# A gated mix of a state-space layer and attention on one core: where VectorE's share of the exponentials is taken from

## The chip, the cores and the metric

The kernel runs on one core of one Trainium2 chip. The metric is the device time of one execution in microseconds (us); the median of three runs is 934.88 (934.81 to 934.90). Its engines are TensorE (PE in the profile, its weight loads PEld), ScalarE (ACT), VectorE (DVE), GpSimd (POOL) and SyncE (SP), which here issues DMAs. Each works through a queue of its own in a fixed order and waits for the others by semaphores.

## The reference

One input `x` of 2048 rows by 1024 columns goes through two layers, and a gate mixes them row by row:

```
x = A_x
g = sigmoid((x * gate_w).sum(-1))            # one number per row
a = 2 Re(C h_t) + x * Dskip,  h_t = Lam_bar * h_(t-1) + B_bar x_t   # complex state, 1024 channels, 2048 steps
q, k, v = split(x @ wqkv)                    # 32 heads of 32
b = softmax(q k^T / sqrt(32)) v @ wo         # no mask
out = g * a + (1 - g) * b
```

Attention has 32 x 2048 x 2048 scores, about 134 million exponentials; they concern this case. Inputs and output are bf16.

## The kernel before

**Bursts.** The 32 heads are worked in 8 groups of four. A group has 8 units, one for each 256 queries, and a unit has 8 bursts, one for each 256 keys: 512 bursts in all. `burst(B)` (L1565 on) writes out one burst. One TensorE operation (QK, L1575) makes the scores of four heads: eight matmuls, for each head two key tiles of 128 keys by 256 queries, transposed so that keys lie on the partitions. A head's 512 columns (key tile 0, then key tile 1) fill one PSUM bank. Banks 0 to 5 are three slots of two banks (names `("S", 0)` to `("S", 2)`); burst number p takes the slots 2p mod 3 and 2p+1 mod 3, the first for heads 0 and 1, the second for heads 2 and 3. The scores of burst p+1 are therefore written over those of the first half of burst p and of the second half of burst p-1, and QK waits until both have been read.

ScalarE turns each half of a burst into exponentials with one ACTIVATE of 1024 columns (L1593) and writes them in bf16 to SBUF (`pt`, and in the opening other tiles that are still free). The numbers are not shifted by a maximum. The value matmuls (`pv`, L1649) follow about two bursts later: for each head, key tile and half of the queries one matmul of 33 columns into bank 6 (32 value columns and one of ones, which gives the sums). They are counted in quarters of a burst, of four matmuls each. After a unit's last quarter `normalize` (L1662, L1663) divides on VectorE.

**VectorE's share.** In some bursts VectorE computes part of the exponentials by bit arithmetic: a multiply and a clamp of the scores into a fixed-point number (`x_in`, L1584), a cubic in its fraction by three operations (`x_q`, L1614, L1615, L1611), and on GpSimd a last multiply and add whose 16-bit result is the bit pattern of the bf16 exponential (`x_p`, L1612). Two bursts make a batch: of bursts 0 and 2, or 4 and 6, of a unit, VectorE takes the last 256 columns of the fourth head, that is its key tile 1. ScalarE's second ACTIVATE is then of 768 columns (L1590), and waits for `x_in`, since both read the same bank. `x_in` stands directly behind QK in the written order; the three operations and GpSimd's come later, out of a list `xbg`. Two extra value operations (`x_pv`, L1629) multiply the batch's 512 columns, at burst 7 of the unit for bursts 0 and 2, at burst 1 of the next unit for bursts 4 and 6. `X_PLAN` names the 72 places, each a multiple of four bursts, at which a batch starts; the first is burst 148.

**What else TensorE does.** Beside attention it has the projections (L1402, L1420), the state-space layer's input product (`u`, L1432), its output product (`c`, L1461, with a diagonal matmul for `Dskip`, L1467) and the output projection (L1492). These dense chains use bank 7, one chain at a time; VectorE empties it at a chain's end (an evacuation). The state-space recurrence itself runs on VectorE as scans (L1349) between elementwise operations.

**The order.** A loop in `build` (from L1734) walks through the bursts and writes every queue in advance. In each burst it puts down QK and the exps, the quarters of value matmuls that are due, about four dense matmuls, and VectorE's background work. For that it keeps an estimate of VectorE's time (`dve_t`) against the burst's planned start `t0`; a burst is planned at 1.83 us, less 0.12 after one in which VectorE takes columns. Work from `xbg` goes ahead of other background work (`bg`, `bg2`) where it can start about as early. What does not end by a limit is left to the next burst. All this is fixed when the kernel is built; on the chip only semaphores decide.

The lines below are those that the diff touches and what calls them.

Of the kernel before, what the change touches and what calls it, by code (L numbers as in the profile page):

```python
# [6 lines left out]
BF = mybir.dt.bfloat16  # L7
F32 = mybir.dt.float32
# [923 lines left out]
RING = 60  # L932
C_LOADS = 28

X_AT = ((0, 2), (4, 6))
X_PLAN = (148, 152, 156, 160, 164, 168, 172, 176, 180, 184, 188, 192, 196, 200, 204, 208, 212, 216, 220, 224, 228, 232, 236, 240, 244, 248, 252, 256, 260, 296, 300, 304, 308, 312, 316, 320, 324, 328, 332, 360, 364, 368, 372, 380, 392, 396, 400, 404, 408, 412, 416, 420, 424, 428, 432, 436, 440, 444, 448, 452, 456, 460, 464, 468, 472, 476, 480, 484, 488, 492, 496, 500)
X_COLS = 256
X_A = SCALE * math.log2(math.e) * 65536.0
X_LO = -127.0 * 65536.0
E3, E2, E1, E0 = 0.0780245226404788, 0.2260671649, 0.6958335355, 0.9999252185627155  # L940
# [13 lines left out]
class FastPath:  # L954

    def __init__(self, nc, S, es, d, flag):
# [28 lines left out]
        self.xi = T("xi", [128, 2 * X_COLS], I32)  # L985
        self.xq = T("xq", [128, 2 * X_COLS], F32)
        self.xp = T("xp", [128, 2 * X_COLS], BF)
# [83 lines left out]
    def begin(self):  # L1071
        S, d = self.S, self.d
        pool, dve, act = self.pool, self.dve, self.act
        warm = self.hpb[0][:, 0, 0, :]
        dve(lambda e: e.memset(warm, 0.0), [], ["warm"])
        self.ld_w(0, 1, "act")
        self.ld_x(0)
        self.ld_w(0, 0, "act")
        for i, nm in enumerate(["A_Lambda_re", "A_Lambda_im", "A_log_dt", "A_Dskip", "gate_w"]):
            self.dma(lambda e, i=i, nm=nm: e.dma_start(self.prow[8 * i:8 * i + 8], d[nm].rearrange("(a p) -> a p", p=128)),  # L1080
                     [], [("prm", i)], "ld_prm", "act")
        for i in range(1, 8):
# [4 lines left out]
        pool(lambda e: e.memset(self.ones, 1.0), [], [("xp", 0)])  # L1087
        pool(lambda e: e.memset(self.badb[:, 1:2], 1.0), [], ["one"])
        pool(lambda e: e.affine_select(self.ident[:], self.ones, pattern=[[1, 128]], base=0, channel_multiplier=-1,
                                       compare_op=ALU.is_equal, fill=0.0), [("xp", 0)], ["ident"])  # L1090
# [472 lines left out]
    def burst(self, B):  # L1563
# [15 lines left out]
        mine = self.x_of.get(B)  # L1579
        first = None  # L1580
        if mine is not None:
            b, n = mine
            s = sl[1]
            first = self.dve(lambda e: e.tensor_scalar(self.xi[:, X_COLS * n:X_COLS * (n + 1)], ps[:, 2 * s + 1, 512 - X_COLS:512], X_A, X_LO, ALU.mult, ALU.max),  # L1584
                             [("S", s)], [("xi", n)], "x_in")
        for z in range(2):
            s, p = sl[z], self.pt_of(B, z)
            if z == 1 and first is not None:
                flat = lambda ap: ap.rearrange("p h n -> p (h n)")[:, 0:1024 - X_COLS]
                self.S.op("act", lambda e, s=s, p=p: e.activation(flat(self.tile[p]), flat(ps[:, 2 * s:2 * s + 2, :]), ACT.Exp, scale=SCALE),  # L1590
                     reads=[("S", s)], writes=[("pt", p)], deps=[first], name="exp")
            else:
                self.act(lambda e, s=s, p=p: e.activation(self.tile[p], ps[:, 2 * s:2 * s + 2, :], ACT.Exp, scale=SCALE), [("S", s)], [("pt", p)], "exp")  # L1593

    def x_plan(self, U, pair):
        self.x_when.setdefault(8 * U + (7 if pair[1] < 4 else 9), []).append(len(self.x_batch))
        for n, i in enumerate(pair):
            self.x_of[8 * U + i] = (len(self.x_batch), n)
        self.x_batch.append([8 * U + i for i in pair])

    def x_ops(self, b):
# [6 lines left out]
        i2, p2 = [("xi", 0), ("xi", 1)], [("xp", 0), ("xp", 1)]  # L1608
# [5 lines left out]
        return [(0.66, 0.0, lambda: self.dve(lambda e: e.scalar_tensor_tensor(xq[:], lo, E2 / E3 * w, lo, ALU.add, ALU.mult), i2, ["xq"], "x_q")),  # L1614
                (0.7, 0.0, lambda: self.dve(lambda e: e.scalar_tensor_tensor(xq[:], xq[:], E1 / E3 * w * w, lo, ALU.add, ALU.mult), ["xq"] + i2, ["xq"], "x_q")),  # L1615
                (0.7, 0.0, last)]

    def x_pv(self, b):

        ps, V = self.ps, self.V  # L1620
        for n, B in enumerate(self.x_batch[b]):
            U, i = divmod(B, BURSTS)
            g = U // QUNITS

            def mm(e, n=n, i=i, g=g):
                m = None
                for qt in range(2):
                    o = 33 * (4 * qt + 3)
                    m = e.matmul(ps[:, 6, o:o + 33], self.xp[:, X_COLS * n + 128 * qt:X_COLS * n + 128 * (qt + 1)], V[:, g % 2, 2 * i + 1, 3, :],  # L1629
                                 start=False, stop=False, skip_group_check=True)  # L1630
                return m
            self.S.op("pe", mm, reads=[("xp", n), ("V", g % 2, i // 2), "v1"], acc=["O"], name="pvx")

    def pv(self, q0, q1):

        ps, V = self.ps, self.V
        for q in range(q0, q1):
# [4 lines left out]

            def mm(e, B=B, z=z, p=p, kl=kl, i=i, g=g):
                m = None
                for h2 in range(1 if z == kl == 1 and B in self.x_of else 2):
                    for qt in range(2):
                        h = 2 * z + h2
                        o = 33 * (4 * qt + h)
# [28 lines left out]
    def build(self):  # L1677
# [13 lines left out]
        self.xbg, self.x_done = [], set()  # L1691
        self.opening()

        S.tok_w["O"] = S.tok_w[("bank", 6)]
# [37 lines left out]
        for p in range(first, NBURST):  # L1732
# [2 lines left out]
            self.p = p  # L1735
            if p > first:
                t0 += period
            if p % 4 == 0 and p in X_PLAN:
                self.x_plan(p // 8, X_AT[p // 4 % 2])
            while p in self.x_of and len(self.xbg) > 1:  # L1740
                self.xbg.pop(0)[2]()
            self.burst(p)
            period = PERIOD - (0.12 if p - 1 in self.x_of else 0.0)
            if p in self.x_of:
                self.dve_t = max(self.dve_t, t0 + 0.45) + 0.42
                b, n = self.x_of[p]
                if n == 1:
                    self.xbg += [[c, wait, f] for c, wait, f in self.x_ops(b)]
            q0, q1 = self.quarters[p]

            def values():
                self.pv(q0, q1)
                for b in self.x_when.get(p, ()):
                    while b not in self.x_done:
                        self.xbg.pop(0)[2]()
# [300 lines left out]
```

## Time and profile before

| | |
|---|---|
| median of three runs | 934.88 us |
| the profiled execution | 934.42 us |
| its span in the profile | 932.7 us |
| ScalarE busy | 916.7 us (98%), 1034 instructions |
| TensorE busy | 886.7 us (95%) |
| its weight loads | 501.7 us (54%) |
| VectorE busy | 718.8 us (77%) |
| GpSimd busy | 56.1 us (6%) |
| granted TensorE clock, mean | 0.998 |

How to read the lines that follow. A row of the groups is a source line, an engine, an operation and the tiles it writes and reads; after the shapes stand the count, then the busy time and the mean length of one in ns, and behind the second bar the engine's idle time just before and what ended most of it. Tiles carry the prefix `f_`. A row of a timeline has start and length in us; neighbours of one kind are merged (x3), so start plus length is the end of the last. Matmul ends are modelled, and a busy TensorE is not one at its peak. An ACTIVATE's row may start before the one ahead of it has ended, since the engine works on both at once.

### The profile page before, as it was taken

What the parts mean: (1) busy time and instruction counts of PE and PEld (TensorE: products, weight loads), DVE (VectorE), ACT (ScalarE), POOL (GpSimd) and SP (SyncE); (2) the same over time, 40 slices, a digit from 0 to 9 for tenths busy, and PEclk for the clock granted to TensorE, in tenths of its full rate; (3) what the DMA queues carried; (4) which work ended last, traced back from release to release, by engine and by line L of the source; (5) the groups of instructions that cost most, each with busy time, mean ns of one, the idle gap of its engine ahead of it and who ended that gap; (6) DMA issues with size and microseconds to landing.
All of it is one profiled execution on the core that took longest, in us unless ns stands there. A gap on an engine that the chain in (4) does not pass through costs nothing.

```text
span 932.7 us, 33715 instructions
## 1 busy us (share of the span) xinstructions
PE 886.7 (95%) x15095; PEld 501.7 (54%) x15316; DVE 718.8 (77%) x1457; ACT 916.7 (98%) x1034; POOL 56.1 (6%) x112
## 2 busy tenths in 40 slices
PE   8899999999999999999999999999999999989995
PEld 4555744464445565555655555544655655545553
DVE  2788888899888999886689965688898655676663
ACT  6999999999999999999999999999999999999997
POOL 2000000000000101100100010100000000001000
PEclk9999999999999999999999999999999999999999
DMA  9559433410233002130022501125201112323312
GB/s 201 96 101 139 76 53 76 84 30 27 42 64 84 31 8 51 41 86 29 8 41 51 86 16 41 42 62 98 42 16 41 53 50 63 121 84 121 119 62 74
DMA packets 157093, 60.90 MB, mean 65 GB/s; under 512 B 145680, under 2 KB 145680, under 8 KB 156944
## 3 DMA queue, kind: packets, MB, share of 16 engines
q1 hardware_dynamic: 154784, 58.16, 28.3%
q8 instruction: 121, 1.98, 0.9%
q10 hardware_dynamic: 2160, 0.53, 0.3%
q14 instruction: 28, 0.23, 0.1%
HBM read 16.79 MB, written 12.58 MB: 31 GB/s over the span
## 4 chain that ended last, share of the span: by engine, by line
ACT 74%; PE 19%; DVE 4%; SPq 1%; issue 1%; DMA 1%; DVEq 0%
ACT f_pt L1593 60%; ACT f_pt L1590 6%; PE f_ps L1461 6%; PE f_ps L1649 4%; PE f_ps L1575 4%; ACT f_OT L1593 2%; ACT f_Et L1593 2%; ACT f_cT_re L1593 2%; ACT f_cT_im L1593 2%; PE f_ps L1420 1%; PE f_ps L1402 1%; SPq L1052 1%; PE f_ps L1432 1%; DVE f_xi L1584 1%; DMA f_xT<-in_A_x_dram 1%
## 5 line engine op out<-in xcount | busy, mean ns | idle before, releaser
L1593 ACT ACTIVATE f_pt<-f_ps 128x1024 bf16<-128x1024 f32 x800 | 757.0, 1154 | 1.0 <-PE f_ps L1575 0.6
L1649 PEld LDWEIGHTS f_ps<-f_V,f_pt 128*128 128x128 bf16 x7264 | 224.0, 96 | 95.4 <-issue 68.4
L1649 PE MATMUL f_ps<-f_V,f_pt 128*128 128x33 bf16 x7264 | 260.1, 178 | 0.4 <-ACT f_pt L1593 0.4
L1575 PE MATMUL f_ps<-f_Q,f_K 32*128 32x256 bf16 x4096 | 203.4, 273 | 19.5 <-ACT f_pt L1593 8.3
L1575 PEld LDWEIGHTS f_ps<-f_Q,f_K 32*128 32x128 bf16 x4096 | 60.8, 92 | 161.6 <-ACT f_pt L1593 134.3
L1590 ACT ACTIVATE f_pt<-f_ps 128x768 bf16<-128x768 f32 x144 | 126.3, 877 | 0.6 <-DVE f_xi L1584 0.5
L1432 PE MATMUL f_ps<-f_xT,f_wb 128*128 128x512 bf16 x448 | 117.7, 379 | 6.3 <-issue 1.1
L1402 PE MATMUL f_ps<-f_xT,f_wb 128*128 128x512 bf16 x406 | 106.7, 379 | 3.9 <-issue 0.2
L1612 POOL TENSOR_SCALAR f_xp<-f_xq 128x512 int16<-128x512 f32 x72 | 46.1, 640 | 617.5 <-DVE f_xq L1611 433.4
L1584 DVE TENSOR_SCALAR f_xi<-f_ps 128x256 int32<-128x256 f32 x144 | 60.7, 422 | 28.7 <-PE f_ps L1575 26.0
L1349 DVE TENSOR_TENSOR_SCAN f_ht<-f_pf,f_init,f_ut 128x512 bf16<-128x512 f32 x64 | 81.0, 1279 | 0.0
L1461 PE MATMUL f_ps<-f_cT_im,f_hp 128*128 128x512 bf16 x192 | 72.6, 378 | 3.1
L1432 PEld LDWEIGHTS f_ps<-f_xT,f_wb 128*128 128x128 bf16 x512 | 40.0, 96 | 38.9 <-issue 7.8
L1420 PE MATMUL f_ps<-f_wb,f_xT 128*128 128x128 bf16 x896 | 59.3, 219 | 0.0
L1492 PE MATMUL f_ps<-f_wb,f_OT 128*128 128x512 bf16 x186 | 55.0, 380 | 2.9 <-DVE f_Et L1498 0.9
L1402 PEld LDWEIGHTS f_ps<-f_xT,f_wb 128*128 128x128 bf16 x464 | 36.1, 96 | 35.7 <-issue 8.0
L1461 PE MATMUL f_ps<-f_cT_re,f_hp 128*128 128x512 bf16 x144 | 54.5, 379 | 0.0
L1662 DVE RECIPROCAL f_rc<-f_ps 128x8 f32<-128x8 f32 x63 | 13.0, 207 | 51.4 <-PE f_ps L1629 38.8
L1420 PEld LDWEIGHTS f_ps<-f_wb,f_xT 128*128 128x128 bf16 x896 | 50.4, 97 | 3.8 <-issue 3.8
L1611 DVE SCALAR_TENSOR_TENSOR f_xq<-f_xi,f_xq 128x512 f32<-128x512 int16 x72 | 49.8, 692 | 2.5
L1614 DVE SCALAR_TENSOR_TENSOR f_xq<-f_xi 128x512 f32<-128x512 uint16 x72 | 49.8, 692 | 2.5
L1615 DVE SCALAR_TENSOR_TENSOR f_xq<-f_xq,f_xi 128x512 f32<-128x512 f32 x72 | 49.8, 692 | 2.4
(147 smaller groups left out, 853.7 us busy)
## 6 DMA issues: line engine op xcount, KB each, us to landing
ag_scratch<-f_Ag SPq DMA_DIRECT2D x32, 256.0 KB, 2.0
f_hp<-ag_scratch SPq DMA_DIRECT2D x32, 256.0 KB, 2.8
f_wb<-in_B_wqkv_dram SPq DMA_DIRECT2D x21, 256.0 KB, 3.9
out_dram<-f_xT SPq DMA_DIRECT2D x16, 256.0 KB, 2.1
f_wb<-in_B_wo_dram SPq DMA_DIRECT2D x2, 768.0 KB, 4.9
f_OT<-f_On SPq DMA_TRANSPOSE x63, 2.3
f_wb<-in_B_wqkv_dram ACTq DMA_DIRECT2D x2, 256.0 KB, 4.2
f_wb<-in_A_B_re_dram SPq DMA_TRANSPOSE x32, 3.5
```

The source lines that it names most:

```text
L1349: ops.append((1.29, lambda ri=ri: dve(lambda e: e.tensor_tensor_scan(ht[:, ri, :], rr, ut[:, ri, :], self.init[:, ri, j:j + 1], ALU.mult, ...
L1402: mms.append((1, lambda e, f, l, a=a: e.matmul(ps[:, bank, :], w[:, g % 2, part, a, :], xT[:, a, 512 * ch:512 * (ch + 1)], start=f, stop=l ...
L1420: m = e.matmul(ps[:, bank, 128 * q:128 * (q + 1)], xT[:, a, 128 * kt:128 * (kt + 1)], w[:, g % 2, 2, a, :], start=(a == 0), stop=(a == 7))
L1432: mms.append((1, lambda e, f, l, a=a: e.matmul(ps[:, 7, :], bT[:, (2 * n + ri) % 3, a, :], xT[:, a, 512 * ch:512 * (ch + 1)], start=f, sto ...
L1461: mms.append((1, lambda e, f, l, j=j, ri=ri: e.matmul(ps[:, 7, :], hp[:, ri, j, cols], cT[ri][:, j, 512 * cb:512 * (cb + 1)], start=f, sto ...
L1492: mms.append((1, lambda e, f, l, j=j: e.matmul(ps[:, 7, :], OT[:, j, 256 * qb + 128 * r:256 * qb + 128 * (r + 1)], wo[j][0][:, 512 * cb:51 ...
L1575: m = e.matmul(ps[:, 2 * sl[h // 2] + h % 2, 256 * kl:256 * (kl + 1)], K[32 * h:32 * h + 32, g % 2, 128 * kt:128 * (kt + 1)], Q[32 * h:32 ...
L1584: first = self.dve(lambda e: e.tensor_scalar(self.xi[:, X_COLS * n:X_COLS * (n + 1)], ps[:, 2 * s + 1, 512 - X_COLS:512], X_A, X_LO, ALU.m ...
L1590: self.S.op("act", lambda e, s=s, p=p: e.activation(flat(self.tile[p]), flat(ps[:, 2 * s:2 * s + 2, :]), ACT.Exp, scale=SCALE), reads=[("S ...
L1593: self.act(lambda e, s=s, p=p: e.activation(self.tile[p], ps[:, 2 * s:2 * s + 2, :], ACT.Exp, scale=SCALE), [("S", s)], [("pt", p)], "exp")
L1611: self.dve(lambda e: e.scalar_tensor_tensor(xq[:], hi, 128.0 / X_K, xq[:], ALU.mult, ALU.add), i2 + ["xq"], ["xq"], "x_q")
L1649: m = e.matmul(ps[:, 6, o:o + 33], self.tile[p][:, h2, 256 * kl + 128 * qt:256 * kl + 128 * (qt + 1)], V[:, g % 2, 2 * i + kl, h, :], star ...
```

## The change

VectorE now takes all 512 columns of the fourth head, both key tiles, from one burst in four, in place of 256 columns from two. That head has a bank of its own, so ScalarE's second ACTIVATE of that burst reads the other bank alone, 512 columns, and does not wait for `x_in`. `x_in` becomes one operation of 512 columns and moves from directly behind QK into the list `xbg`, where it is planned no earlier than 0.45 us after the burst's planned start; it is put down at the latest before the burst that writes over its slot. The three further operations and GpSimd's keep their size, as does the number of such blocks, 72. The extra value matmuls come as one operation of four, at burst 6 of the unit for burst 0 and at burst 1 of the next unit for burst 4. New bookkeeping (`x_got`, `x_out`, `x_free`, `x_flush`) keeps a batch's last step from being written down before the earlier batch's value matmuls. The planned period is 0.11 us shorter in each of the four bursts after the start of such a block. Two of the 72 places move, from 256 and 260 to 284 and 292.

```
-X_AT = ((0, 2), (4, 6))
-X_PLAN = (148, ..., 252, 256, 260, 296, ..., 500)
-X_COLS = 256
+X_PLAN = (148, ..., 252, 284, 292, 296, ..., 500)
+X_LAST = 0.71
...
     def burst(self, B):
...
-        if mine is not None:
-            b, n = mine
-            s = sl[1]
-            first = self.dve(lambda e: e.tensor_scalar(self.xi[:, X_COLS * n:X_COLS * (n + 1)], ps[:, 2 * s + 1, 512 - X_COLS:512], X_A, X_LO, ALU.mult, ALU.max),
-                             [("S", s)], [("xi", n)], "x_in")
         for z in range(2):
             s, p = sl[z], self.pt_of(B, z)
-            if z == 1 and first is not None:
-                flat = lambda ap: ap.rearrange("p h n -> p (h n)")[:, 0:1024 - X_COLS]
-                self.S.op("act", lambda e, s=s, p=p: e.activation(flat(self.tile[p]), flat(ps[:, 2 * s:2 * s + 2, :]), ACT.Exp, scale=SCALE),
-                     reads=[("S", s)], writes=[("pt", p)], deps=[first], name="exp")
+            if z == 1 and B in self.x_of:
+                self.act(lambda e, s=s, p=p: e.activation(self.tile[p][:, 0, :], ps[:, 2 * s, :], ACT.Exp, scale=SCALE), [("S", s)], [("pt", p)], "exp")
+                self.xbg += [[c, wait, f] for c, wait, f in self.x_ops(self.x_of[B], ps[:, 2 * s + 1, :], s)]
...
+    def x_plan(self, B):
+        U, i = divmod(B, BURSTS)
+        self.x_when.setdefault(8 * U + (6 if i < 4 else 9), []).append(len(self.x_batch))
...
     def x_ops(self, b, src, s):
+        def into():
+            self.dve(lambda e: e.tensor_scalar(xi[:], src, X_A, X_LO, ALU.mult, ALU.max), [("S", s)], i2, "x_in")
+            self.x_got.add(b)
...
+        return [(0.7, 0.45, into),
...
+    def x_free(self):
+        return len(self.x_done) == self.x_out
+
+    def x_flush(self):
+        c, wait, f = self.xbg.pop(0)
+        assert self.x_free() or c != X_LAST
+        f()
+        self.dve_t += c
...
     def pv(self, q0, q1):
-                for h2 in range(1 if z == kl == 1 and B in self.x_of else 2):
+                for h2 in range(1 if z == 1 and B in self.x_of else 2):
...
     def build(self):
-            if p % 4 == 0 and p in X_PLAN:
-                self.x_plan(p // 8, X_AT[p // 4 % 2])
-            while p in self.x_of and len(self.xbg) > 1:
-                self.xbg.pop(0)[2]()
+            if p in X_PLAN:
+                self.x_plan(p)
+            while p - 2 in self.x_of and self.x_of[p - 2] not in self.x_got:
+                self.x_flush()
             self.burst(p)
-            period = PERIOD - (0.12 if p - 1 in self.x_of else 0.0)
+            period = PERIOD - (0.11 if any(p - k in self.x_of for k in range(1, 5)) else 0.0)
             if p in self.x_of:
-                self.dve_t = max(self.dve_t, t0 + 0.45) + 0.42
-                b, n = self.x_of[p]
-                if n == 1:
-                    self.xbg += [[c, wait, f] for c, wait, f in self.x_ops(b)]
+                x_t = t0
...
-                if self.xbg:
+                if self.xbg and (self.xbg[0][0] != X_LAST or self.x_free()):
```

More of the change, by code (lines that the diff above doesn't have):

```diff
@@ L933 @@
 C_LOADS = 28
[L935 to L937 removed]
+X_PLAN = (148, 152, 156, 160, 164, 168, 172, 176, 180, 184, 188, 192, 196, 200, 204, 208, 212, 216, 220, 224, 228, 232, 236, 240, 244, 248, 252, 284, 292, 296, 300, 304, 308, 312, 316, 320, 324, 328, 332, 360, 364, 368, 372, 380, 392, 396, 400, 404, 408, 412, 416, 420, 424, 428, 432, 436, 440, 444, 448, 452, 456, 460, 464, 468, 472, 476, 480, 484, 488, 492, 496, 500)
+X_LAST = 0.71
 X_A = SCALE * math.log2(math.e) * 65536.0
@@ L984, in __init__ @@
         self.tq = T("tq", [128, 2, 512], BF)
-        self.xi = T("xi", [128, 2 * X_COLS], I32)
-        self.xq = T("xq", [128, 2 * X_COLS], F32)
-        self.xp = T("xp", [128, 2 * X_COLS], BF)
+        self.xi = T("xi", [128, 512], I32)
+        self.xq = T("xq", [128, 512], F32)
+        self.xp = T("xp", [128, 512], BF)
         self.ut = T("ut", [128, 2, 512], F32)
@@ L1086, in begin @@
         act(lambda e: e.activation(self.cm[:, 0, 0:1], warm[:, 0:1], ACT.Exp), ["warm"], [("cm", 0)], "table")
-        pool(lambda e: e.memset(self.ones, 1.0), [], [("xp", 0)])
+        pool(lambda e: e.memset(self.ones, 1.0), [], ["xp"])
         pool(lambda e: e.memset(self.badb[:, 1:2], 1.0), [], ["one"])
         pool(lambda e: e.affine_select(self.ident[:], self.ones, pattern=[[1, 128]], base=0, channel_multiplier=-1,
-                                       compare_op=ALU.is_equal, fill=0.0), [("xp", 0)], ["ident"])
+                                       compare_op=ALU.is_equal, fill=0.0), ["xp"], ["ident"])
         flat = lambda r0, r1: self.pf[:, r0:r1, :].rearrange("p a b -> p (a b)")
@@ L1578, in burst, with x_ops @@
         self.S.op("pe", mm, reads=[("K", g % 2, i // 2), ("Q", qz)], writes=[("S", sl[0]), ("S", sl[1])], name="qk")
-        mine = self.x_of.get(B)
-        first = None
-        if mine is not None:
-            b, n = mine
-            s = sl[1]
-            first = self.dve(lambda e: e.tensor_scalar(self.xi[:, X_COLS * n:X_COLS * (n + 1)], ps[:, 2 * s + 1, 512 - X_COLS:512], X_A, X_LO, ALU.mult, ALU.max),
-                             [("S", s)], [("xi", n)], "x_in")
         for z in range(2):
             s, p = sl[z], self.pt_of(B, z)
-            if z == 1 and first is not None:
-                flat = lambda ap: ap.rearrange("p h n -> p (h n)")[:, 0:1024 - X_COLS]
-                self.S.op("act", lambda e, s=s, p=p: e.activation(flat(self.tile[p]), flat(ps[:, 2 * s:2 * s + 2, :]), ACT.Exp, scale=SCALE),
-                     reads=[("S", s)], writes=[("pt", p)], deps=[first], name="exp")
+            if z == 1 and B in self.x_of:
+                self.act(lambda e, s=s, p=p: e.activation(self.tile[p][:, 0, :], ps[:, 2 * s, :], ACT.Exp, scale=SCALE), [("S", s)], [("pt", p)], "exp")
+                self.xbg += [[c, wait, f] for c, wait, f in self.x_ops(self.x_of[B], ps[:, 2 * s + 1, :], s)]
             else:
                 self.act(lambda e, s=s, p=p: e.activation(self.tile[p], ps[:, 2 * s:2 * s + 2, :], ACT.Exp, scale=SCALE), [("S", s)], [("pt", p)], "exp")
[L1595 to L1601, printed above, removed]
+    def x_plan(self, B):
+        U, i = divmod(B, BURSTS)
+        self.x_when.setdefault(8 * U + (6 if i < 4 else 9), []).append(len(self.x_batch))
+        self.x_of[B] = len(self.x_batch)
+        self.x_batch.append(B)
+    def x_ops(self, b, src, s):
         xi, xq, xp = self.xi, self.xq, self.xp
@@ L1607, in x_ops @@
         w = 65536.0
-        i2, p2 = [("xi", 0), ("xi", 1)], [("xp", 0), ("xp", 1)]
+        i2, p2 = ["xi"], ["xp"]
+        def into():
+            self.dve(lambda e: e.tensor_scalar(xi[:], src, X_A, X_LO, ALU.mult, ALU.max), [("S", s)], i2, "x_in")
+            self.x_got.add(b)
         def last():
@@ L1613, in last, with mm @@
             self.x_done.add(b)
-        return [(0.66, 0.0, lambda: self.dve(lambda e: e.scalar_tensor_tensor(xq[:], lo, E2 / E3 * w, lo, ALU.add, ALU.mult), i2, ["xq"], "x_q")),
+        return [(0.7, 0.45, into),
+                (0.7, 0.0, lambda: self.dve(lambda e: e.scalar_tensor_tensor(xq[:], lo, E2 / E3 * w, lo, ALU.add, ALU.mult), i2, ["xq"], "x_q")),
                 (0.7, 0.0, lambda: self.dve(lambda e: e.scalar_tensor_tensor(xq[:], xq[:], E1 / E3 * w * w, lo, ALU.add, ALU.mult), ["xq"] + i2, ["xq"], "x_q")),
-                (0.7, 0.0, last)]
+                (X_LAST, 0.0, last)]
+    def x_free(self):
[5 more added lines that the diff above has]
+        self.dve_t += c
     def x_pv(self, b):
         ps, V = self.ps, self.V
[L1621 to L1626, printed above, removed]
+        B = self.x_batch[b]
+        U, i = divmod(B, BURSTS)
+        g = U // QUNITS
+        def mm(e):
+            m = None
+            for kl in range(2):
                 for qt in range(2):
                     o = 33 * (4 * qt + 3)
-                    m = e.matmul(ps[:, 6, o:o + 33], self.xp[:, X_COLS * n + 128 * qt:X_COLS * n + 128 * (qt + 1)], V[:, g % 2, 2 * i + 1, 3, :],
+                    m = e.matmul(ps[:, 6, o:o + 33], self.xp[:, 256 * kl + 128 * qt:256 * kl + 128 * (qt + 1)], V[:, g % 2, 2 * i + kl, 3, :],
                                  start=False, stop=False, skip_group_check=True)
-                return m
-            self.S.op("pe", mm, reads=[("xp", n), ("V", g % 2, i // 2), "v1"], acc=["O"], name="pvx")
+            return m
+        self.x_out += 1
+        self.S.op("pe", mm, reads=["xp", ("V", g % 2, i // 2), "v1"], acc=["O"], name="pvx")
     def pv(self, q0, q1):
@@ L1690, in build @@
         self.x_of, self.x_batch, self.x_when = {}, [], {}
-        self.xbg, self.x_done = [], set()
+        self.xbg, self.x_got, self.x_done, self.x_out = [], set(), set(), 0
         self.opening()
@@ L1754, in values @@
                     while b not in self.x_done:
-                        self.xbg.pop(0)[2]()
+                        self.x_flush()
                     self.x_pv(b)
```

## The prediction

> **What bounds the kernel now.** I read the page first, for the engine that sets the pace and for the chain of waits that ended last.
>
> ```profile
> span 932.7 us, 33715 instructions
> PE 886.7 (95%) x15095; PEld 501.7 (54%) x15316; DVE 718.8 (77%) x1457; ACT 916.7 (98%) x1034; POOL 56.1 (6%) x112
> ACT 74%; PE 19%; DVE 4%; SPq 1%; issue 1%; DMA 1%; DVEq 0%
> ```
>
> ScalarE is busy for 98% of the span and carries 74% of the chain; TensorE is close behind. What matters is how the two hand over in a burst, so next come the groups, with shapes kept apart: the pieces that the change touches, and three that I use as prices.
>
> ```profile
> L1593 ACT ACTIVATE f_pt<-f_ps 128x1024 bf16<-128x1024 f32 x800 | 757.0, 1154 | 1.0 <-PE f_ps L1575 0.6
> L1590 ACT ACTIVATE f_pt<-f_ps 128x768 bf16<-128x768 f32 x144 | 126.3, 877 | 0.6 <-DVE f_xi L1584 0.5
> L1584 DVE TENSOR_SCALAR f_xi<-f_ps 128x256 int32<-128x256 f32 x144 | 60.7, 422 | 28.7 <-PE f_ps L1575 26.0
> L1349 DVE TENSOR_TENSOR_SCAN f_ht<-f_pf,f_init,f_ut 128x512 bf16<-128x512 f32 x64 | 81.0, 1279 | 0.0
> L1474 DVE TENSOR_SCALAR f_Ag<-f_ps,f_gcol 128x512 f32<-128x512 f32 x32 | 24.0, 750 | 22.0 <-PE f_ps L1461 21.3
> L1409 DVE CAST f_K<-f_ps 128x512 bf16<-128x512 f32 x28 | 19.3, 691 | 7.4 <-PE f_ps L1402 6.7
> L1629 PE MATMUL f_ps<-f_V,f_xp 128*128 128x33 bf16 x288 | 18.4, 178 | 0.0
> ```
>
> Idle time of ScalarE is almost nil by this view (1.0 and 0.6 us), but that hides something: an ACTIVATE's row starts before its forerunner's has ended, so a short gap shows as a smaller overlap. I therefore compare ends. Here is the timeline of ScalarE alone (start, length, line, shape, count).
>
> ```profile
> 304.84 0.81 ACT L1590 ACTIVATE f_pt<-f_ps 128x768 bf16<-128x768 f32 x1
> 308.35 0.83 ACT L1590 ACTIVATE f_pt<-f_ps 128x768 bf16<-128x768 f32 x1
> 309.19 1.02 ACT L1593 ACTIVATE f_pt<-f_ps 128x1024 bf16<-128x1024 f32 x1
> ...
> 319.45 2.95 ACT L1593 ACTIVATE f_pt<-f_ps 128x1024 bf16<-128x1024 f32 x3
> 322.18 0.92 ACT L1590 ACTIVATE f_pt<-f_ps 128x768 bf16<-128x768 f32 x1
> 322.92 2.93 ACT L1593 ACTIVATE f_pt<-f_ps 128x1024 bf16<-128x1024 f32 x3
> 325.65 0.91 ACT L1590 ACTIVATE f_pt<-f_ps 128x768 bf16<-128x768 f32 x1
> 326.36 2.95 ACT L1593 ACTIVATE f_pt<-f_ps 128x1024 bf16<-128x1024 f32 x3
> 329.09 0.92 ACT L1590 ACTIVATE f_pt<-f_ps 128x768 bf16<-128x768 f32 x1
> ```
>
> The runs of three end at 322.40, 325.85 and 329.31, the short exps at 323.10, 326.56 and 330.01. So, end to end, three full exps take 2.75 us (0.917 each) and a 768-column one 0.70; 256 columns are worth 0.21, and a 512-column exp would be 0.917 - 0.42 = 0.49. A full exp on an emptied ScalarE (309.19, the forerunner having ended at 309.18) takes 1.02. When ScalarE alone sets the pace, a full burst is 1.833, one with a short exp 0.70 + 0.917 = 1.62, and a block of four bursts, two of them short, 3.667 + 3.24 = 6.91.
>
> Now the handover. Scores of burst p+1 (QK, L1575) overwrite the banks of the first exp of burst p (three slots of two banks in rotation), so they wait for that exp. The whole timeline at the burst that started the last row above:
>
> ```profile
> 327.63 0.40 PE L1575 MATMUL f_ps<-f_Q,f_K 32*128 32x256 bf16 x8
> 328.08 0.42 DVE L1584 TENSOR_SCALAR f_xi<-f_ps 128x256 int32<-128x256 f32 x1
> 329.36 0.40 PE L1575 MATMUL f_ps<-f_Q,f_K 32*128 32x256 bf16 x8
> 329.81 2.03 ACT L1593 ACTIVATE f_pt<-f_ps 128x1024 bf16<-128x1024 f32 x2
> ```
>
> The first exp ends at 329.31 (above), QK starts 0.05 later, the next first exp can start 0.45 after that, and ends at the earliest 1.02 after its start. So from the end of one burst's first exp to the end of the next one's there is a floor of 0.05 + 0.45 + 1.02 = **1.52 us**, whatever the second exp costs. A short burst of before, 1.62, stays above it by 0.10: that spare absorbs some lateness of TensorE, and a full burst (1.833) has 0.31 of it.
>
> What the blocks really take, from the 768-column rows at the ends of two stretches in which every block has such exps, and of two pieces of them:
>
> ```profile
> 283.85 1.01 ACT L1590 ACTIVATE f_pt<-f_ps 128x768 bf16<-128x768 f32 x1
> 478.82 0.88 ACT L1590 ACTIVATE f_pt<-f_ps 128x768 bf16<-128x768 f32 x1
> 714.66 1.11 ACT L1590 ACTIVATE f_pt<-f_ps 128x768 bf16<-128x768 f32 x1
> 903.54 0.89 ACT L1590 ACTIVATE f_pt<-f_ps 128x768 bf16<-128x768 f32 x1
> ...
> 381.18 0.83 ACT L1590 ACTIVATE f_pt<-f_ps 128x768 bf16<-128x768 f32 x1
> 423.53 0.83 ACT L1590 ACTIVATE f_pt<-f_ps 128x768 bf16<-128x768 f32 x1
> 841.39 0.88 ACT L1590 ACTIVATE f_pt<-f_ps 128x768 bf16<-128x768 f32 x1
> ```
>
> By their ends: 28 blocks in 194.84 and 27 in 188.66, mean 6.973. The last nine (842.27 to 904.43) take 6.907 each, which is ScalarE's own pace; the mean block loses 0.066 against it. Six in the middle (382.01 to 424.36) take 7.06: those are bursts whose dense work is a C product. The timeline of TensorE shows why:
>
> ```profile
> 423.81 0.40 PE L1575 MATMUL f_ps<-f_Q,f_K 32*128 32x256 bf16 x8
> 425.57 0.40 PE L1575 MATMUL f_ps<-f_Q,f_K 32*128 32x256 bf16 x8
> 427.27 0.40 PE L1575 MATMUL f_ps<-f_Q,f_K 32*128 32x256 bf16 x8
> 429.12 0.40 PE L1575 MATMUL f_ps<-f_Q,f_K 32*128 32x256 bf16 x8
> ...
> 434.23 0.40 PE L1575 MATMUL f_ps<-f_Q,f_K 32*128 32x256 bf16 x8
> 435.93 0.40 PE L1575 MATMUL f_ps<-f_Q,f_K 32*128 32x256 bf16 x8
> ```
>
> With 16 value matmuls and four dense ones a burst costs TensorE 1.70 (434.23 to 435.93), in a C product with its diagonal matmul 1.76 (423.81 to 425.57), and with four value matmuls of VectorE's tile on top 1.85 (427.27 to 429.12), that is 0.1 more. Four C bursts make 4 x 1.76 = 7.04, so there TensorE is the bound by a little. The counts of the diagonal matmuls in the stretches with short exps (columns: stretch, length, busy and count of TensorE, of its loads, clock, DMA) give 108, four to a block: 27 of the 72 blocks lie in C products.
>
> ```profile
> 283.00:487.00 204.00, 9.61 (x44) 4.25 (x44) 1.00 0.18 43
> 543.00:615.00 72.00, 6.99 (x32) 3.09 (x32) 1.00 0.14 43
> 657.00:687.00 30.00, 0.00 (x0) 0.00 (x0) 1.00 0.14 24
> 713.00:913.00 200.00, 6.99 (x32) 3.09 (x32) 1.00 0.26 80
> ```
>
> The other 45 come to (72 x 6.97 - 27 x 7.06) / 45 = 6.92.
>
> **The change, part by part.**
>
> *ScalarE.* Per block, two exps of 768 become one of 1024 and one of 512. Columns and instruction count stay equal, so its own work stays 6.91: 3 x 1.833 + 0.49 + 0.917. But the floor now bites: the burst with the 512-column exp wants 0.49 + 0.917 = 1.41 and gets 1.52. All four banks' scores come from one QK operation that waits for the first exp, and nothing in the diff changes that. Price: 0.11 a block. From both sides: 0 if some queueing on ScalarE hid it, against which stands 309.19, where the length after a wait is already the shortest; and 0.21 if TensorE came 0.1 late there as in 427.27 to 429.12. I take 0.11, the value of the rows in which nobody was late. New block: 3 x 1.833 + 1.52 = 7.02.
>
> *Quiet blocks.* 45 x (7.02 - 6.92) = **+4.5 us**. Does lateness of TensorE add to it? After the stalled burst it needs 1.70 where 1.52 is allowed and is 0.18 late; the four extra value matmuls make it 0.28; each of the three full bursts gives back 0.13, so nothing is left when the next 512-column exp comes.
>
> *C blocks.* TensorE needs 1.76, is 0.24 late, 0.34 with the extra matmuls, and regains only 0.07 a burst: about 0.1 is left at the next short burst, where it adds to 7.02. So 7.06 to 7.14 against 7.06 now; I take the middle, 7.10: 27 x 0.04 = **+1.1 us** (0 to 2.2).
>
> *VectorE.* Two reads of 256 columns (2 x 422 ns) become one of 512: 0.69 to 0.75 by the 512-column PSUM rows of L1409 and L1474, so it is relieved of 0.09 to 0.15 a block, some 7 to 11 us in all. VectorE has idle time (77% busy), and the wait of an exp for its read, which falls away, was 0.5 us in all. The 26.0 us in which its read stood waiting for QK were idle time of VectorE; what stood behind it there could only matter through late evacuations, which are among the 4.8 us (72 x 0.066) that the blocks now lose in all. I take 0.
>
> *The read's new place.* It goes from straight behind QK into the background queue, with 512 columns of slots to free before QK of burst p+2. That is due about 0.45 + 1.02 + 1.52 = 3.0 us after the burst's QK starts; at 0.7 us long it may start 2.3 after it, against 0.45 now (327.63, 328.08). One scan of 1.28 ahead of it fits. A scan, an evacuation (0.69) and a normalization ahead do not: it would be some 0.8 late, and QK with it. Zero to perhaps eight of 72 events, 0 to +6 us; I take 0, since the planner puts this queue first.
>
> *TensorE, GpSimd, DMA.* Four value matmuls go and four come (L1629, L1649) per block, as now, in one operation instead of two; GpSimd's step keeps its 512 columns. No DMA is added or moved. Two blocks move from bursts 256 and 260 to 284 and 292; nothing before burst 148 (283 us) changes. The shorter planned period shifts background work by one burst here or there: 0, between -1 and +1 us.
>
> Sum: +4.5 + 1.1 = +5.6 us. The profiled execution took 934.42 us (span 932.7 and 1.7 around it), 0.46 under the median of 934.88, so I forecast 940.0 for such an execution and **940.5 us** for the median.
>
> The Trainium skill prices the step otherwise: its page "ScalarE: Activation LUTs", section "What ACT_TABLE_LOAD costs", gives an ACTIVATE 186 ns plus 0.833 ns per column alone and lets neighbours overlap by about 93 ns. As an estimate by that page, a full exp is 1.04 alone and 0.95 in a row, a 512-column one 0.52, and the stall 0.50 + 1.04 - 0.95 - 0.52 = 0.07, which over 45 quiet blocks would make the sum some 1.8 us smaller, 938.7. The trace has 0.917 in a row over many exps and 1.02 alone, and it decides.
>
> **The rivals.**
>
> *No stall: faster.* If ScalarE finds the next scores ready after 0.49, a block costs its own 6.91 everywhere, and with late reads gone the present loss of 0.066 a block vanishes: 934.9 - 4.8 = 930.1. For it: all ScalarE work fits in 6.91, and VectorE and ScalarE no longer take turns in a bank. Against: the 0.05 and 0.45 on each side of QK at 329.36. It decides where the stall is under 0.066 a block; near that value the time stays at 934.9, which I count as a case of its own. The Trainium skill, "Perfetto Trace Analysis", section "Matmuls", says that independent matmul groups should rotate through PSUM banks so that one's evacuation overlaps the next one's matmuls; by that rule this case would come true, but here the rotation of three slots already makes QK wait for the first exp, whichever engine reads the second.
>
> *Late reads: slower still.* VectorE's read slips behind evacuation and normalization in several blocks; at 0.8 each, five of them give 944.5. For it: the scan's 1279 ns and a VectorE that is busy for 77% of the span. Against: 1.8 us more room than now.
>
> **How the numbers follow.** The stall as priced 0.70 (938.5 to 942: C blocks 0 to 2.2, quiet ones 0.02 either way, planning 1 us); late reads on top 0.17 (942 to 947); no net change 0.06; no stall 0.07. Range 937.5 to 944.5: it leaves out the last two and the far end of the late reads. A measurement of this kernel can tell about 0.2% (1.9 us) from no change: faster 0.07, same 0.06, slower 0.87.
>
> **What would show it.** In the new profile the exp after each 512-column one starts about 0.50 after the end of its burst's first exp and lasts 1.02; runs of blocks outside the C products take 7.02 by ends, against 6.91 in the last stretch now; idle of ScalarE before L1593 stays tiny in the groups or grows by under 0.1 a block; VectorE loses 7 to 11 us. I am wrong if blocks take 6.91 (QK earlier than I think), or if QK is seen waiting for VectorE's read.

## The result

The changed kernel takes a median of 939.42 us (938.79 to 940.92) against 934.85 us (934.25 to 935.67) of the kernel before in the same comparison: a ratio of 1.005, 95% interval 1.0037 to 1.0063. It is 4.6 us slower, where I had forecast 5.6; 939.42 lies in the range and in the case that I held likeliest.

The page of the changed kernel: its span, the engines' busy times, the chain that ended last by engine, and the groups that answer to those shown of before (the second exp of a short burst is now L1581, VectorE's read L1602, QK L1574).

```profile
span 937.7 us, 33727 instructions
PE 889.6 (95%) x15095; PEld 502.9 (54%) x15316; DVE 708.0 (75%) x1385; ACT 920.8 (98%) x1034; POOL 59.7 (6%) x112
ACT 89%; PE 7%; SPq 1%; DVE 1%; DMA 1%; issue 0%; DVEq 0%
...
L1584 ACT ACTIVATE f_pt<-f_ps 128x1024 bf16<-128x1024 f32 x872 | 808.7, 1131 | 1.8 <-PE f_ps L1574 0.6
L1602 DVE TENSOR_SCALAR f_xi<-f_ps 128x512 int32<-128x512 f32 x72 | 49.3, 685 | 11.4 <-PE f_ps L1574 9.8
L1581 ACT ACTIVATE f_pt<-f_ps 128x512 bf16<-128x512 f32 x72 | 49.4, 685 | 0.0
```

VectorE is relieved of 10.8 us (718.8 to 708.0), as worked out, and the kernel is slower all the same. The share of ScalarE in the chain has gone from 74% to 89%, although its columns are the same: TensorE, 19% of the chain before, is down to 7%. Idle time of ScalarE, 1.8 us here, again shows nothing of the loss.

The handover shows it. The timeline of the changed kernel at one of its short exps:

```profile
844.31 1.09 ACT L1584 ACTIVATE f_pt<-f_ps 128x1024 bf16<-128x1024 f32 x1
845.22 0.67 ACT L1581 ACTIVATE f_pt<-f_ps 128x512 bf16<-128x512 f32 x1
845.45 0.40 PE L1574 MATMUL f_ps<-f_Q,f_K 32*128 32x256 bf16 x8
845.90 1.02 ACT L1584 ACTIVATE f_pt<-f_ps 128x1024 bf16<-128x1024 f32 x1
```

The first exp of the burst ends at 845.40. QK starts 0.05 later, the next first exp 0.45 after that, and it takes the 1.02 us of an emptied ScalarE: 1.52 us from end to end, though the short exp had ended at 845.89. As its forerunner's end and its own start lie 0.01 us apart, the row shows no idle time; what is lost is the overlap that neighbours have otherwise.

And it repeats. In the chain of the changed kernel, in order of time (start, length, what), the pieces on ScalarE are runs of seven full exps:

```profile
831.85 6.52 ACT f_pt L1584 x7
838.88 6.52 ACT f_pt L1584 x7
852.93 6.52 ACT f_pt L1584 x7
859.96 6.52 ACT f_pt L1584 x7
```

6.52 is 1.02 + 6 x 0.917. Each run begins 7.03 us after the one before (14.05 for two), with 0.51 between them for QK and the waits on its two sides. In 70 of the 72 blocks with a short exp it is the same 7.03 (7.11 in the other two):

| mean block, us | before | after |
|---|---|---|
| 24 blocks in C products | 7.019 | 7.034 |
| 42 quiet blocks | 6.934 | 7.027 |
| 6 blocks at a border | 7.018 | 7.027 |
| all 72 | 6.969 | 7.029 |

(From the end of a block's first exp to the end of the next block's first exp; the kernel before decides which place is of which kind: a C block has a diagonal matmul in at least three of its bursts, one at a border in two, a quiet one in none.) From burst 148 to burst 505 that is 628.30 us before and 632.59 after, 4.29 of the 5.0 us between the two spans. 0.73 of the rest lies ahead of burst 16, where the two kernels are the same, so it is no work of the change: the end of that burst's first exp lies anywhere from 40.95 to 42.93 us in the profiles of this case.

The mean of the quiet blocks before hides one thing. Of the 42, 39 take 6.91 (6.905 to 6.936), ScalarE's own pace. The other three, from burst 452 to 463, take 7.11, 7.64 and 7.03, together 1.05 us more than the 39 do, and VectorE was late in them. From the timeline of the kernel before, where the most was lost:

```profile
829.91 0.69 DVE L1505 TENSOR_TENSOR f_Et<-f_Et 128x512 bf16<-128x512 f32 x1
830.52 0.42 DVE L1584 TENSOR_SCALAR f_xi<-f_ps 128x256 int32<-128x256 f32 x1
830.97 0.81 ACT L1590 ACTIVATE f_pt<-f_ps 128x768 bf16<-128x768 f32 x1 [0.50 <-DVE f_xi L1584]
```

The short exp stood for 0.50 us until VectorE had read the bank that both read. In the changed kernel no exp waits for that read, and the three blocks take 7.027 like the others.

### The profile page after: what moved, and what is told of

The parts are those of the page before. It is cut to its first block, busy times and chain, and to the rows that moved or that the text cites. A ratio compares the mean times of both kernels' runs of the same rounds, so it can differ in the third digit from the quotient of the medians.

```text
span 937.7 us, 33727 instructions
## 1 busy us (share of the span) xinstructions
PE 889.6 (95%) x15095; PEld 502.9 (54%) x15316; DVE 708.0 (75%) x1385; ACT 920.8 (98%) x1034; POOL 59.7 (6%) x112
## 4 chain that ended last, share of the span: by engine, by line
ACT 89%; PE 7%; SPq 1%; DVE 1%; DMA 1%; issue 0%; DVEq 0%
ACT f_pt L1584 79%; ACT f_pt L1581 3%; PE f_ps L1460 2%; ACT f_OT L1584 2%; ACT f_Et L1584 2%; ACT f_cT_re L1584 2%; PE f_ps L1656 2%; ACT f_cT_im L1584 2%; PE f_ps L1574 1%; SPq L1051 1%; DMA f_xT<-in_A_x_dram 1%; PE f_ps L1431 1%; PE f_ps L1401 0%; PE f_ps L1466 0%; PE f_ps L1172 0%
## 5 line engine op out<-in xcount | busy, mean ns | idle before, releaser
L1584 ACT ACTIVATE f_pt<-f_ps 128x1024 bf16<-128x1024 f32 x872 | 808.7, 1131 | 1.8 <-PE f_ps L1574 0.6
L1574 PE MATMUL f_ps<-f_Q,f_K 32*128 32x256 bf16 x4096 | 203.3, 273 | 21.7 <-ACT f_pt L1584 8.4
L1574 PEld LDWEIGHTS f_ps<-f_Q,f_K 32*128 32x128 bf16 x4096 | 61.0, 92 | 164.4 <-ACT f_pt L1584 123.1
L1607 POOL TENSOR_SCALAR f_xp<-f_xq 128x512 int16<-128x512 f32 x72 | 49.5, 687 | 671.0 <-DVE f_xq L1606 442.2
L1473 DVE TENSOR_SCALAR f_Ag<-f_ps,f_gcol 128x512 f32<-128x512 f32 x32 | 24.0, 750 | 56.9 <-PE f_ps L1460 56.8
L1602 DVE TENSOR_SCALAR f_xi<-f_ps 128x512 int32<-128x512 f32 x72 | 49.3, 685 | 11.4 <-PE f_ps L1574 9.8
L1581 ACT ACTIVATE f_pt<-f_ps 128x512 bf16<-128x512 f32 x72 | 49.4, 685 | 0.0
```

Of the source, the lines that this page charges most:

```text
L1574: m = e.matmul(ps[:, 2 * sl[h // 2] + h % 2, 256 * kl:256 * (kl + 1)], K[32 * h:32 * h + 32, g % 2, 128 * kt:128 * (kt + 1)], Q[32 * h:32 ...
L1581: self.act(lambda e, s=s, p=p: e.activation(self.tile[p][:, 0, :], ps[:, 2 * s, :], ACT.Exp, scale=SCALE), [("S", s)], [("pt", p)], "exp")
```

## The experiments

My theory was the floor: the scores of the next burst wait for the first exp of this one, so a burst cannot fall under 0.05 + 0.45 + 1.02 = 1.52 us, and ScalarE cannot use what a 512-column exp saves over one of about 640 columns (0.60 us after 0.917). The rivals: ScalarE's own work sets the pace; TensorE does; VectorE's read, which now comes later, does. In the comparisons that follow the kernel before took between 934.97 and 935.22 us, so a difference from the 939.42 of the changed kernel is good to about 0.4 us.

### A shorter exp still

```
-                self.act(lambda e, s=s, p=p: e.activation(self.tile[p][:, 0, :], ps[:, 2 * s, :], ACT.Exp, scale=SCALE), [("S", s)], [("pt", p)], "exp")
+                self.act(lambda e, s=s, p=p: e.activation(self.tile[p][:, 0, 0:256], ps[:, 2 * s, 0:256], ACT.Exp, scale=SCALE), [("S", s)], [("pt", p)], "exp")
```

> The changed kernel with the short exp cut from 512 to 256 columns; key tile 1 of the third head is left out there (stale numbers are multiplied instead). ScalarE has 0.21 us less work a block, 15 us in all. Handover theory: the burst stays at 1.53, block 7.03, time within 0.5 us of the changed kernel. Rival, ScalarE's work sets the time: 924.

It took 939.22 us (938.42 to 940.90), as the changed kernel, though ScalarE was spared 72 x 256 columns and was busy for 905.6 us in place of 920.8. It leaves out those columns of the third head. Its timeline at the same burst as above:

```profile
845.20 0.46 ACT L1581 ACTIVATE f_pt<-f_ps 128x256 bf16<-128x256 f32 x1
845.43 0.40 PE L1574 MATMUL f_ps<-f_Q,f_K 32*128 32x256 bf16 x8
845.88 2.86 ACT L1584 ACTIVATE f_pt<-f_ps 128x1024 bf16<-128x1024 f32 x3 [0.23 <-PE f_ps L1574]
```

Measured from QK, the exp ends 0.21 earlier, and ScalarE now stands visibly idle for 0.23 us, waiting for QK; the next exp starts 0.45 after QK as ever, and the mean block is 7.028. That excludes ScalarE's own work as the bound of these bursts.

### QK in two parts

```
-        def mm(e):
+        def mm(e, hs=range(4)):
...
-                for h in range(4):
+                for h in hs:
...
-        self.S.op("pe", mm, reads=[("K", g % 2, i // 2), ("Q", qz)], writes=[("S", sl[0]), ("S", sl[1])], name="qk")
+        if B - 1 in self.x_of:
+            for z in range(2):
+                self.S.op("pe", lambda e, z=z: mm(e, (2 * z, 2 * z + 1)), reads=[("K", g % 2, i // 2), ("Q", qz)], writes=[("S", sl[z])], name="qk")
+        else:
+            self.S.op("pe", mm, reads=[("K", g % 2, i // 2), ("Q", qz)], writes=[("S", sl[0]), ("S", sl[1])], name="qk")
```

The burst behind a short exp thus has its scores written for heads 0 and 1 first, then for heads 2 and 3.

> The changed kernel, but the QK operation of the burst behind each 512-column exp is written as two: heads 0 and 1 first, then heads 2 and 3. The first waits only for the slot that was read a burst earlier, the second for the first exp of the burst ahead. Handover theory: the next first exp no longer waits for that exp's end plus QK, the 0.11 to 0.12 us of stall goes, a block falls from 7.03 towards ScalarE's own 6.91, 5 to 8 us less than the changed kernel (931 to 934). Rival 1, ScalarE simply needs that long for a 512-column exp and what follows: no change (939.4). Rival 2, TensorE is the bound: QK in two halves keeps half of its row groups idle, costs about 0.1 to 0.2 a block, 940 to 950.

It took 935.58 us (934.53 to 936.86), 3.8 under the changed kernel (4.2 when each is taken against the kernel before in its own comparison) and level with the kernel before (ratio 1.0001, 0.9991 to 1.0010). The direction was as expected, the size fell short of 5 to 8. By the same measure as in the table, quiet blocks fell from 7.027 to 6.935 and C blocks stayed at 7.034. From the timeline of the split kernel: the short exps at both ends of the last nine blocks (841 and 903 us), and between them the handover at one of these (848 us):

```profile
841.28 0.67 ACT L1585 ACTIVATE f_pt<-f_ps 128x512 bf16<-128x512 f32 x1
...
848.18 0.69 ACT L1585 ACTIVATE f_pt<-f_ps 128x512 bf16<-128x512 f32 x1
848.40 0.42 PE L1574 MATMUL f_ps<-f_Q,f_K 32*128 32x256 bf16 x8
848.75 0.60 PE L1491 MATMUL f_ps<-f_wb,f_OT 128*128 128x512 bf16 x2
848.83 4.69 ACT L1588 ACTIVATE f_pt<-f_ps 128x1024 bf16<-128x1024 f32 x5
...
903.72 0.69 ACT L1585 ACTIVATE f_pt<-f_ps 128x512 bf16<-128x512 f32 x1
```

By ends, the nine blocks take (904.41 - 841.95) / 9 = 6.94, against 7.027 in the changed kernel and 6.907 before. So the wait of the whole QK for the first exp is most of what the quiet blocks lost: 0.09 of the 0.12 by which 7.027 stands above ScalarE's own 6.907. In what is left the next exp still follows QK (848.83, 0.43 behind 848.40), so I put it down to TensorE, which comes late to QK; the last experiment bears on that.

### The same split in the kernel before

The same edit as in the last diff, for the bursts behind each 768-column exp.

> The kernel before, with QK of the burst behind each 768-column exp written as two operations (heads 0 and 1, then heads 2 and 3), as in the split of the changed kernel. Handover theory: its short bursts of 1.62 us stay above the floor of 1.53 anyway, so in quiet blocks there is nothing to win, and the split costs TensorE some 0.05 to 0.1 a time: 935 to 939, against the 3.9 us that the same split took off the changed kernel. Rival, splitting QK helps any burst because ScalarE gets its scores earlier: 1 to 4 us faster than before.

935.88 us (934.89 to 937.01), ratio 1.0007 (0.9997 to 1.0016): nothing won. Quiet blocks are at 6.932 against 6.934. A burst of 1.62 stays above the floor, and the split has nothing to remove; that speaks against the reading that any earlier score helps.

### TensorE relieved, in both kernels

Both kernels leave out the value matmuls of VectorE's columns, and with them that part of the sums. In the changed kernel:

```
-        self.S.op("pe", mm, reads=["xp", ("V", g % 2, i // 2), "v1"], acc=["O"], name="pvx")
```

In the kernel before, to the same end:

```
-        for n, B in enumerate(self.x_batch[b]):
+        for n, B in enumerate([]):
```

> The kernel before without the value matmuls of VectorE's columns (288 of 33 columns; that part of the sums is left out). TensorE has 0.1 us less a block. If its lateness makes the 7.06 of the C blocks, they fall by 0.05 to 0.1, quiet blocks stay at 6.91: 1.5 to 3 us faster than before. Rival, VectorE's read in front of the short exp makes the loss: no change.

> The changed kernel without the value matmuls of VectorE's columns (288 of 33 columns, left out of the sums). Handover theory: nearly every block stands at the floor of 7.03 already, TensorE's relief is worth nothing there: within 0.5 us of the changed kernel. Rival, TensorE's 7.03 a C block is as much the bound as the handover: 1 to 3 us faster.

The kernel before fell to 932.63 us (931.28 to 934.62; ratio 0.9976, 0.9966 to 0.9985), 2.5 us; its C blocks went from 7.019 to 6.925, its quiet ones from 6.934 to 6.929. These are the ends of the six middle blocks that the prediction had at 7.06, in the kernel before without these matmuls:

```profile
381.08 0.85 ACT L1590 ACTIVATE f_pt<-f_ps 128x768 bf16<-128x768 f32 x1
422.83 0.83 ACT L1590 ACTIVATE f_pt<-f_ps 128x768 bf16<-128x768 f32 x1
```

(423.66 - 381.93) / 6 = 6.955. The changed kernel without them stayed at 939.28 us (938.92 to 939.71), every kind of block at 7.026 to 7.027. So before, TensorE was the bound of the C blocks; in the changed kernel, where TensorE and the floor ask for nearly the same 7.03, taking TensorE's part away frees nothing.

### VectorE's read: first, late, twice

Read first, by an operation directly behind QK, with an empty one in its place in the planner's list:

```
-                self.xbg += [[c, wait, f] for c, wait, f in self.x_ops(self.x_of[B], ps[:, 2 * s + 1, :], s)]
+                ops = self.x_ops(self.x_of[B], ps[:, 2 * s + 1, :], s)
...
+                ops[0][2]()
+                self.xbg += [[0.7, 0.45, lambda: None]] + [[c, wait, f] for c, wait, f in ops[1:]]
```

> The changed kernel with VectorE's 512-column read put back directly behind QK in the written order; the planner's costs and all else stay. Handover theory: no QK waits for the read in either kernel, so the time stays within 1 us of the changed kernel. Rival, the read's later place costs part of the 4.6 us: up to 4 us faster. Rival the other way, VectorE waiting for QK delays evacuations: 1 to 3 us slower.

939.39 us (938.82 to 940.87): no difference. Where the read stands costs the changed kernel nothing.

Read late:

```
-        return [(0.7, 0.45, into),
+        return [(0.7, 2.2, into),
```

> The changed kernel with VectorE's read planned no earlier than 2.2 us after the burst's planned start in place of 0.45; the planner then puts other work ahead of it. By my working a read that starts later than 2.3 us after QK makes the QK two bursts on late. Theory: in a good part of the 72 blocks it does, 0.3 to 1 us each, 10 to 40 us slower than the changed kernel. Rival, there is much more room than I worked out: within 2 us of it.

1003.68 us (1002.57 to 1004.25), 64 us over the changed kernel; I had expected 10 to 40. The waits of TensorE in it (who waited for whom: us in total, times, longest):

```profile
PE f_ps L1574 <- DVE f_xi L1602: 65.7, 54, 2.6
PE f_ps L1574 <- ACT f_pt L1584: 6.9, 24, 0.7
```

In 54 blocks QK waited for the read, 1.2 us on average. The wait is real, and the room for the read is limited as worked out; the planner with its 0.45 keeps well inside it, and in the changed kernel no QK is seen waiting for the read.

Read twice in a row:

```
             self.dve(lambda e: e.tensor_scalar(xi[:], src, X_A, X_LO, ALU.mult, ALU.max), [("S", s)], i2, "x_in")
+            self.dve(lambda e: e.tensor_scalar(xi[:], src, X_A, X_LO, ALU.mult, ALU.max), [("S", s)], i2, "x_in")
```

> The changed kernel with VectorE's 512-column read done twice in a row, 72 x 0.69 = 49 us more of VectorE work, the planner not told. If VectorE's relief is worth nothing, as I priced it, its load costs little too: within 2 us of the changed kernel. Rival, VectorE's time matters through late evacuations and slots: 5 us or more slower.

947.15 us (946.61 to 947.82), 7.7 us slower than the changed kernel: a miss. From its timeline, where a block lost much:

```profile
388.29 1.28 DVE L1348 TENSOR_TENSOR_SCAN f_ht<-f_pf,f_init,f_ut 128x512 bf16<-128x512 f32 x1
...
390.16 0.40 PE L1574 MATMUL f_ps<-f_Q,f_K 32*128 32x256 bf16 x8
390.49 0.57 PE L1657 MATMUL f_ps<-f_V,f_pt 128*128 128x33 bf16 x16
390.58 0.74 DVE L1473 TENSOR_SCALAR f_Ag<-f_ps,f_gcol 128x512 f32<-128x512 f32 x1
391.38 0.39 PE L1460 MATMUL f_ps<-f_cT_re,f_OT 128*128 128x512 bf16 x1 [0.32 <-DVE f_Ag L1473]
...
392.40 0.40 PE L1574 MATMUL f_ps<-f_Q,f_K 32*128 32x256 bf16 x8
```

VectorE, behind its plan, empties bank 7 only at 391.32. TensorE's next dense chain starts at 391.38, and QK, which stands behind it, 2.24 us after the last one. The waits of TensorE's weight loads name a second path:

```profile
PEld f_ps L1657 <- DVE f_On L1671: 11.9, 33, 0.6
```

Here value matmuls wait until `normalize` has read bank 6; in the changed kernel no value matmul waits for it. Of some 8 us by which bursts of these blocks are late, about 3.5 lie in 12 bursts with a dense chain that waited for an evacuation, 2.2 in 24 bursts with value matmuls that waited for a normalization, and 2.4 in bursts without such a wait, where the lateness seems to be carried on. None of TensorE's waits is for the read itself. So 49 us more of VectorE cost 7.7 us, by late evacuations and late normalizations.

### The first half of QK earlier

To take lateness of TensorE out of the split kernel as well, heads 0 and 1 of the burst behind a short exp were written behind the third dense matmul of the burst ahead, and heads 2 and 3 at QK's old place.

```
+            ahead = p in self.x_of
...
                 f()
                 used += wt
+                if used == 3 and wt and ahead:
+                    ahead = False
+                    self.burst(p + 1, True)
...
+            if ahead:
+                self.burst(p + 1, True)
```

Either call writes the first half of the next burst's QK and nothing else; the second stands for bursts that have no third dense matmul.

> The changed kernel with the split QK, and the first half (heads 0 and 1) written earlier in TensorE's queue, behind the third dense matmul of the burst ahead, so that lateness of TensorE no longer holds back the first exp after a 512-column one. Handover theory: quiet blocks go from 6.935 with the split alone to ScalarE's own 6.91, C blocks stay at 7.03 (TensorE's work): 1 to 2 us less than the split alone, 933.5 to 934.5, 0 to 2 us under the kernel before. Rival, the half operations and the changed order cost TensorE as much as they win: 935 to 937.

960.04 us (959.18 to 960.48; ratio 1.0264, 1.0250 to 1.0278): 20.6 us slower than the changed kernel, far outside both what I had expected and its rival. The timeline of TensorE shows what the half operation costs:

```profile
451.84 0.40 PE L1575 MATMUL f_ps<-f_Q,f_K 32*128 32x256 bf16 x8
452.17 0.57 PE L1666 MATMUL f_ps<-f_V,f_pt 128*128 128x33 bf16 x16
...
453.35 0.39 PE L1575 MATMUL f_ps<-f_Q,f_K 32*128 32x256 bf16 x4
453.67 0.40 PE L1419 MATMUL f_ps<-f_wb,f_xT 128*128 128x128 bf16 x4
...
454.00 0.39 PE L1575 MATMUL f_ps<-f_Q,f_K 32*128 32x256 bf16 x4
454.32 0.37 PE L1666 MATMUL f_ps<-f_V,f_pt 128*128 128x33 bf16 x8
```

Eight matmuls of QK hold TensorE for 0.33 us (451.84 to 452.17), four of them for 0.32 just as well. Each half set apart costs what a whole QK costs, 0.32 x 72 = 23 us of an engine that has next to no spare.

By ends, the run also confirms the floor. The burst with the 512-column exp falls to 1.407 us in the mean, ScalarE's own 1.41: with its scores there in time, nothing of the stall is left. The burst behind it pays, with 2.228 in place of 1.832, and there ScalarE waits for QK:

```profile
ACT f_pt L1594 <- PE f_ps L1575: 20.4, 57, 0.6
```

No version that computes the whole output beats the kernel before.

## Why the prediction was right, and where it was off

*The floor*, the step that carries the forecast, came out to a hundredth: the burst with the 512-column exp takes 1.530 us in the mean (1.528 in quiet blocks, 1.535 in C blocks), the quiet block 7.027 against my 7.02, and every prediction on its lines held (0.50 from the first exp's end to the next exp's start, a length of 1.02, 7.02 by ends in quiet stretches, hardly any idle time). The two experiments on both sides confirm it: less work for ScalarE changes nothing, a wait less gives back most of what the quiet blocks lost.

*Quiet blocks*, +4.5: they lost 42 x (7.027 - 6.934) = 3.9. That is two things: 39 blocks went from 6.909 to 7.027, which cost 4.6 us, and the three that VectorE had held up gave back 0.7. The price of the stall, 0.11, was right within a hundredth. The mean from which I started was 0.014 too low (6.92, got by subtracting C blocks that were taken too dear), and the count was three too high.

*C blocks*, +1.1: this is the term that was mis-sized. They lost 24 x 0.015 = 0.4. I had taken six of them, at 7.06, for all; the mean was 7.019. And the 7.10 that I gave them afterwards held an error: I added 0.1 us for the extra value matmuls to a burst of 16 value matmuls, but the burst in which the block's own value matmuls are done has four fewer. TensorE is then late by 1.76 - 1.53 = 0.23 and regains 0.07 in each of three full bursts, so that next to nothing is left behind the first exp of the next short one; the trace has a mean of 0.00 (quiet) to 0.01 (C) there. On the way it has TensorE late by 0.18, 0.16 and 0.08 in the mean C block.

The chip sided with the trace's prices of an ACTIVATE: the stall of the short burst over ScalarE's own work is 1.53 - 1.41 = 0.12, where the estimate by the Trainium skill's page "ScalarE: Activation LUTs", section "What ACT_TABLE_LOAD costs", had been 0.07.

*VectorE*, priced at 0: not quite. The prediction counted the wait of the exp for its read by ScalarE's idle time, 0.5 us in all; by ends, VectorE's lateness cost three quiet blocks 1.05 us, and that is gone. They stay as long, at 7.11, 7.53 and 7.03, when TensorE alone is relieved in the kernel before, and take 6.91 in the split kernel. Whether the 10.8 us by which VectorE is relieved were worth anything beyond that is hard to tell. That VectorE's time is worth nothing was wrong as a general statement, as reading twice shows; 49 us more cost 7.7, so by that price 10.8 us less would be worth up to 10.8 x 7.7 / 49 = 1.7, an estimate. No run took just that relief away, so it stays open.

*The read's new place*, priced at 0: right, since putting it first again changes nothing. *No stall* and *no net change* did not come true. For the first, the rule of the Trainium skill's page "Perfetto Trace Analysis", section "Matmuls", would have needed all scores of the next burst to be free of the first exp's banks; where the split frees the half that the next exp reads, the quiet blocks do come back to 6.935.

## What to carry to other kernels

Where two engines hand buffers back and forth, as ScalarE and TensorE do here, look for the chain from one's end through the other and back: no step of the cycle can be shorter than that, however little work the busier one has in it. A saving concentrated in one step was lost below that floor (1.41 wanted, 1.53 got), while the same saving spread over two steps was kept (1.62 each). Compare ends, not idle time: ScalarE, whose instructions overlap, lost 0.12 us in each of 72 blocks, and the idle time in front of its exps hardly grew (from 1.6 to 1.8 us over the two groups). And before work is moved off the bound, look at how much spare the hand-over has at that very place.

## What was not expected of the hardware

A group of QK's matmuls between full-height ones cost TensorE 0.32 to 0.33 us whether it held eight matmuls or four. By the kernel's text each head's 32 rows get two of them either way, and only the number of heads at work side by side differs (eight rows of 273 ns each take 0.40 together). The two halves back to back cost hardly more than one whole: at 848.40 the next dense matmul starts 0.35 behind them. VectorE, idle for a quarter of the span, still passed on 16% of extra work (7.7 of 49 us) to the end, through late evacuations of the bank that the dense chains share and late normalizations.
